# Fourier mixing and a squared-ReLU MLP: the second side of each block transposed one step later, and another end for the last block

## The chip, the cores and the metric

The kernel runs on one core of a Trainium2 chip. The metric is the device time of one execution in microseconds (us), lower is better. Results were compared with the reference.

Engines: PE is TensorE, PEld its weight loads, DVE is VectorE, ACT is ScalarE, POOL is GpSimd, SP is SyncE. A "q" after the name means the engine's instruction queue, which issues DMAs and waits.

## The reference

```python
def _attn_ref(x):                      # x: (8, 3008, 256) float32
    X = np.fft.fft(x, axis=1)
    X = np.fft.fft(X, axis=2)
    return X.real.astype(np.float32)

def _moe_ref(x, w_in, w_out):          # x: (24064, 256), w_in: (256, 2048), w_out: (2048, 256)
    h = x @ w_in
    r = np.maximum(h, 0.0)
    g = r * r
    return (g @ w_out).astype(np.float32)
```

## The kernel before

The kernel uses symmetry: row k and row S-k of a batch are computed together, as two "sides" of one block of up to 251 positions k. There are 48 blocks (8 batches of 6). Each takes 8 steps; a step makes hidden features (`front`: tiles ph), squares them, and multiplies them with the second weights (`back`: seven products into four accumulators mA to mD, a fast 2x2 scheme). While one batch goes through, the folds and DFT products (tiles pd) of the next are slipped in between as side work.

After the eighth step `gather` forms the two sides in `c`, and two steps later `store` transposes them to rows and writes them out:

```python
    psd = ctx.enter_context(tc.tile_pool(name="psd", bufs=2, space=PSUM))   # tag "d": pd tiles AND po tiles
    ...
    def gather(n):
        ...
        nc.scalar.copy(sA[:, :, 0:n], mA[:, :, 0:n])
        nc.scalar.copy(sB[:, :, 0:n], mB[:, :, 0:n])
        m1, m2, m4, m5 = sA[:, 0, 0:n], sA[:, 1, 0:n], sB[:, 0, 0:n], sB[:, 1, 0:n]
        ...
        tt(out=u2, in0=m1, in1=mC[:, 0, 0:n], op=ALU.add)          # VectorE
        tt(out=u3, in0=u2, in1=mC[:, 1, 0:n], op=ALU.add)
        tt(out=u4, in0=u2, in1=mD[:, 0, 0:n], op=ALU.add)
        gt = nc.gpsimd.tensor_tensor
        gt(out=c[:, 0, 0, 0:n], in0=m1, in1=m2, op=ALU.add)        # GpSimd
        gt(out=c[:, 1, 0, 0:n], in0=u3, in1=m4, op=ALU.subtract)
        gt(out=c[:, 1, 1, 0:n], in0=u3, in1=m5, op=ALU.add)
        gt(out=c[:, 0, 1, 0:n], in0=u4, in1=m5, op=ALU.add)
        return c

    def store(b, k0, n, c):
        m = (n + 1) // 2
        starts = (0, n - m)
        ...
        for s, (row, lo, hi) in enumerate(...):                     # both sides, one after the other
            po = psd.tile([P, 2, D], F32, name="po", tag="d")
            for i, o in enumerate(starts):
                for h in range(2):
                    nc.tensor.transpose(po[0:m, i, h * H:(h + 1) * H], c[:, s, h, o:o + m], ident)
            os_ = op.tile([P, 2, D], F32, name="os", tag="os")
            nc.scalar.copy(os_[0:m], po[0:m])
            for i, (o, c0, c1) in enumerate(((0, lo, m), (starts[1], m, hi))):
                nc.sync.dma_start(out=out[row + c0:row + c1], in_=os_[c0 - o:c1 - o, i])
    ...
    for i in range(len(steps) + LAG + 3):
        ...  front of step i, with side work between
        while finished and finished[0][0] <= i:
            store(*finished.pop(0)[1:])
        ...  back of step i - LAG
            if at[3] == NJ - 1:
                finished.append((i + 2, *at[:3], gather(at[2])))
```

## Time and profile before

| | before |
|---|---|
| time, median of 6 runs | 2067.1 us (2064.0 to 2071.0) |
| span of the profiled run | 2062.1 us |
| PE busy | 2004.4 us, 97% |
| PE's idle waits for ScalarE at the transposes | 10.1 us in 15 waits |
| first row of transposes to the last product | 1903.8 us |
| last product to the end of the span | 11.6 us |

The last two rows divide the span into the part that PE fills and the tail after it. What comes before the first transposes (the start: weights are loaded and converted) took 146.7 us in this run and isn't touched by the change.

### The profile page before, as it was taken

The numbers are of one execution on the slowest core, as the hardware profiler recorded it, in microseconds if no ns is written. First come the engines' busy times: TensorE is split into PE (matmuls) and PEld (weight loads), VectorE is DVE, ScalarE is ACT, GpSimd is POOL, SyncE is SP. The second block draws the span as 40 slices with busy tenths as digits, with TensorE's granted clock in tenths as the row PEclk, the third lists the DMA queues.
The fourth block names the chain that finished last, engine by engine and source line by source line (L and its number), as shares of the span: only waits on it lengthen the run. The fifth ranks groups of instructions, "written<-read, shape, count | busy, mean of one in ns | idle before, by whom it ended". The sixth has DMA issues, their size and how long they took to land.

```text
span 2062.1 us, 27082 instructions
## 1 busy us (share of the span) xinstructions
PE 2004.4 (97%) x9464; PEld 1742.7 (85%) x9464; DVE 1335.1 (65%) x3271; ACT 949.4 (46%) x1069; POOL 1204.8 (58%) x1766
## 2 busy tenths in 40 slices
PE   6699999999999999999999999999999999999997
PEld 4588888888888888888888888888888888888887
DVE  6898666776567755677557765677656775555553
ACT  1554444444444544454444444444444454445443
POOL 0376555666556654676557664666655665456565
PEclk9899999999999999999999999999999999999999
DMA  6232000110011010011001100011001100000000
GB/s 177 92 69 49 21 11 31 41 36 21 11 41 41 26 31 25 26 38 39 11 26 36 38 28 11 30 41 36 21 11 40 41 11 21 26 11 11 21 11 20
DMA packets 66104, 68.45 MB, mean 33 GB/s; under 512 B 26297, under 2 KB 56969, under 8 KB 65968
## 3 DMA queue, kind: packets, MB, share of 16 engines
q1 hardware_dynamic: 65152, 66.46, 11.3%
q8 instruction: 74, 1.21, 0.2%
q14 instruction: 62, 0.51, 0.1%
q10 hardware_dynamic: 816, 0.26, 0.1%
HBM read 42.03 MB, written 24.68 MB: 32 GB/s over the span
## 4 chain that ended last, share of the span: by engine, by line
PE 95%; DVE 3%; DMA 1%; ACT 1%; issue 0%; POOL 0%; POOLq 0%; SPq 0%; ACTq 0%; DVEq 0%
PE ph L405 16%; PE mA L445 16%; PE mC L445 16%; PE ph L406 16%; PE mB L445 16%; PE mD L445 8%; PE pd L345 5%; PE po L479 2%; PE pg L229 1%; DMA xt<-in_x_dram 1%; ACT os L481 0%; DVE he L408 0%; DVE fd L211 0%; DVE fs L213 0%; DVE g L411 0%
## 5 line engine op out<-in xcount | busy, mean ns | idle before, releaser
L419 ACT ACTIVATE g<-g 128x1004 f32<-128x1004 f32 (+1 forms) x384 | 399.4, 1040 | 829.3 <-DVE g L411 554.8
L408 DVE SCALAR_TENSOR_TENSOR he<-Et,gE,ph 128x251 f32<-128x251 f32 (+1 forms) x768 | 362.1, 472 | 590.2 <-PE ph L406 589.7
L425 POOL TENSOR_TENSOR s<-g 128x251 f32<-128x251 f32 (+1 forms) x384 | 251.5, 655 | 683.3 <-ACT g L420 656.6
L405 PE MATMUL ph<-Pt,G 128*128 128x251 f32 (+1 forms) x1536 | 452.5, 375 | 0.4 <-DVE g L411 0.4
L406 PE MATMUL ph<-Qt,G 127*128 127x251 f32 (+1 forms) x1536 | 451.2, 374 | 0.0
L420 ACT ACTIVATE g<-g 128x1004 f32<-128x1004 f32 (+1 forms) x384 | 399.3, 1040 | 12.2
L445 PE MATMUL mA<-g,wout 128*128 128x251 f32 (+1 forms) x1536 | 389.4, 375 | 0.0
L445 PE MATMUL mC<-s,wsum 128*128 128x251 f32 (+1 forms) x1536 | 389.4, 374 | 0.0
L410 DVE TENSOR_TENSOR g<-he,ph 128x251 f32<-128x251 f32 (+1 forms) x768 | 320.6, 417 | 58.9 <-DVE he L408 0.5
L405 PEld LDWEIGHTS ph<-Pt,G 128*128 128x128 f32 x1536 | 287.8, 189 | 42.2 <-issue 3.2
L406 PEld LDWEIGHTS ph<-Qt,G 127*128 127x128 f32 x1536 | 291.2, 190 | 35.8
L445 PEld LDWEIGHTS mC<-s,wsum 128*128 128x128 f32 x1536 | 291.6, 190 | 35.2
L445 PEld LDWEIGHTS mA<-g,wout 128*128 128x128 f32 x1536 | 285.0, 189 | 39.7 <-issue 4.0
L411 DVE TENSOR_TENSOR g<-he,ph 128x251 f32<-128x251 f32 (+1 forms) x768 | 314.2, 409 | 0.0
L426 POOL TENSOR_TENSOR s<-s,g 128x251 f32<-128x251 f32 (+1 forms) x384 | 288.8, 752 | 30.1
L427 POOL TENSOR_TENSOR s<-g 128x251 f32<-128x251 f32 (+1 forms) x384 | 290.2, 756 | 0.0
L428 POOL TENSOR_TENSOR s<-g,s 128x251 f32<-128x251 f32 (+1 forms) x384 | 264.2, 688 | 0.0
L445 PE MATMUL mB<-g,wsum 128*128 128x251 f32 (+1 forms) x768 | 225.2, 374 | 0.0
L445 PE MATMUL mD<-s,wout 128*128 128x251 f32 (+1 forms) x768 | 225.0, 374 | 0.0
L445 PE MATMUL mB<-s,wout 128*128 128x251 f32 (+1 forms) x768 | 224.6, 374 | 0.0
L445 PEld LDWEIGHTS mB<-g,wsum 128*128 128x128 f32 x768 | 145.6, 190 | 17.7
L445 PEld LDWEIGHTS mD<-s,wout 128*128 128x128 f32 x768 | 144.9, 189 | 18.1
(73 smaller groups left out, 1317.1 us busy)
## 6 DMA issues: line engine op xcount, KB each, us to landing
xt<-in_x_dram SPq DMA_DIRECT2D x24, 512.0 KB
out_dram<-os SPq DMA_DIRECT2D x96, 125.0 KB
out_dram<-os SPq DMA_DIRECT2D x80, 126.0 KB
xt<-in_x_dram SPq DMA_DIRECT2D x16, 384.0 KB
Et<-e_dram SPq DMA_DIRECT2D x7, 752.5 KB
raw<-in_moe_w_in_dram SPq DMA_DIRECT2D x16, 256.0 KB
raw<-in_moe_w_out_dram SPq DMA_DIRECT2D x16, 256.0 KB
xt<-in_x_dram SPq DMA_DIRECT2D x8, 480.0 KB
```

The source lines that it names most:

```text
L405: nc.tensor.matmul(hP, G1[:, fs], pt[:, ks], start=True, stop=True)
L406: nc.tensor.matmul(hQ, G2[:, fs], qt[:, ks], start=True, stop=True)
L408: nc.vector.scalar_tensor_tensor(out=t, in0=et[:, ks], scalar=gE[:, fc:fc + 1], in1=hP, op0=ALU.mult, op1=ALU.add)
L410: tt(out=g[:, h, 0, 0:n], in0=t, in1=hQ, op=ALU.add)
L411: tt(out=g[:, h, 1, 0:n][:, ::-1], in0=t, in1=hQ, op=ALU.subtract)
L419: act(v, v, AF.Relu)
L420: act(v, v, AF.Square)
L425: gt(out=s1, in0=g21, in1=g22, op=ALU.add)
L426: gt(out=s2, in0=s1, in1=g11, op=ALU.subtract)
L427: gt(out=s3, in0=g11, in1=g21, op=ALU.subtract)
L428: gt(out=s4, in0=g12, in1=s2, op=ALU.subtract)
L445: nc.tensor.matmul(acc[nm][:, i, 0:n], w, v[:, 0:n], start=j == 0 and i == 0, stop=j == NJ - 1, skip_group_check=True)
```

## The change

The intent: no longer let PE wait in the middle of the transposes, and shorten the chain after the last product, when nothing else is left to hide it. There are two independent parts.

Part one gives each side its own entry, so that side two is transposed one step after side one:

```diff
-                finished.append((i + 2, *at[:3], gather(at[2])))
+                c_ = gather(at[2], final)
+                finished += [(i + 2 + s, *at[:3], s, c_, final) for s in range(2)]
```

Part two concerns the last block only (`final`). Its last step makes mB's products at the end; VectorE adds mB straight from PSUM in place of GpSimd with a copy; ScalarE copies side one and issues its stores itself, VectorE copies side two, and the sync engine issues those stores:

```diff
+        if final and j == NJ - 1:
+            products = products[0:2] + products[4:7] + products[2:4]
...
-        nc.scalar.copy(sB[:, :, 0:n], mB[:, :, 0:n])
+        if not final:
+            nc.scalar.copy(sB[:, :, 0:n], mB[:, :, 0:n])
...
         gt(out=c[:, 0, 0, 0:n], in0=m1, in1=m2, op=ALU.add)
+        if final:
+            tt(out=c[:, 0, 1, 0:n], in0=u4, in1=mB[:, 1, 0:n], op=ALU.add)
+            tt(out=c[:, 1, 1, 0:n], in0=u3, in1=mB[:, 1, 0:n], op=ALU.add)
+            tt(out=c[:, 1, 0, 0:n], in0=u3, in1=mB[:, 0, 0:n], op=ALU.subtract)
+            return c
...
-            nc.scalar.copy(os_[0:m], po[0:m])
+        (nc.vector.tensor_copy if final and s else nc.scalar.copy)(os_[0:m], po[0:m])
-                nc.sync.dma_start(out=out[row + c0:row + c1], in_=os_[c0 - o:c1 - o, i])
+            (nc.scalar if final and not s else nc.sync).dma_start(out=out[row + c0:row + c1], in_=os_[c0 - o:c1 - o, i])
```

More of the change, by code (lines that the diff above doesn't have):

```diff
@@ L431, with back @@
     acc = {}
-    def back(n, j, g, s):
+    def back(n, j, g, s, final):
         if j == 0:
@@ L437, in back, with gather @@
                 acc[nm] = psm.tile([P, 2, CH], F32, name=nm, tag=nm)
-        for nm, i, w, v in (("mA", 0, wout[:, 0, j, 0:H], g[:, 0, 0]),
-                            ("mA", 1, wout[:, 1, j, 0:H], g[:, 1, 0]),
-                            ("mB", 0, wsum[:, 2, j], g[:, 1, 1]),
-                            ("mB", 1, wout[:, 0, j, H:D], s[:, 0]),
-                            ("mC", 0, wsum[:, 0, j], s[:, 1]),
-                            ("mC", 1, wsum[:, 1, j], s[:, 2]),
-                            ("mD", 0, wout[:, 1, j, H:D], s[:, 3])):
+        products = [("mA", 0, wout[:, 0, j, 0:H], g[:, 0, 0]),
+                    ("mA", 1, wout[:, 1, j, 0:H], g[:, 1, 0]),
+                    ("mB", 0, wsum[:, 2, j], g[:, 1, 1]),
+                    ("mB", 1, wout[:, 0, j, H:D], s[:, 0]),
+                    ("mC", 0, wsum[:, 0, j], s[:, 1]),
+                    ("mC", 1, wsum[:, 1, j], s[:, 2]),
+                    ("mD", 0, wout[:, 1, j, H:D], s[:, 3])]
+        if final and j == NJ - 1:
+            products = products[0:2] + products[4:7] + products[2:4]
+        for nm, i, w, v in products:
             nc.tensor.matmul(acc[nm][:, i, 0:n], w, v[:, 0:n], start=j == 0 and i == 0, stop=j == NJ - 1,
                              skip_group_check=True)
-    def gather(n):
+    def gather(n, final):
         mA, mB, mC, mD = (acc[nm] for nm in ("mA", "mB", "mC", "mD"))
@@ L467, in gather, with store @@
         return c
-    def store(b, k0, n, c):
+    def store(b, k0, n, s, c, final):
         m = (n + 1) // 2
         starts = (0, n - m)
-        first, last = k0 == 0, k0 + n == NKT
-        for s, (row, lo, hi) in enumerate(((b * S + k0, 0, n),
-                                           (b * S + S - (k0 + n - 1), 1 if last else 0, n - 1 if first else n))):
-            po = psd.tile([P, 2, D], F32, name="po", tag="d")
-            for i, o in enumerate(starts):
-                for h in range(2):
-                    nc.tensor.transpose(po[0:m, i, h * H:(h + 1) * H], c[:, s, h, o:o + m], ident)
-            os_ = op.tile([P, 2, D], F32, name="os", tag="os")
-            nc.scalar.copy(os_[0:m], po[0:m])
-            for i, (o, c0, c1) in enumerate(((0, lo, m), (starts[1], m, hi))):
-                nc.sync.dma_start(out=out[row + c0:row + c1], in_=os_[c0 - o:c1 - o, i])
+        if s == 0:
+            row, lo, hi = b * S + k0, 0, n
+        else:
+            row, lo, hi = b * S + S - (k0 + n - 1), 1 if k0 + n == NKT else 0, n - 1 if k0 == 0 else n
+        po = psd.tile([P, 2, D], F32, name="po", tag="d")
+        for i, o in enumerate(starts):
+            for h in range(2):
+                nc.tensor.transpose(po[0:m, i, h * H:(h + 1) * H], c[:, s, h, o:o + m], ident)
+        os_ = op.tile([P, 2, D], F32, name="os", tag="os")
+        (nc.vector.tensor_copy if final and s else nc.scalar.copy)(os_[0:m], po[0:m])
+        for i, (o, c0, c1) in enumerate(((0, lo, m), (starts[1], m, hi))):
+            (nc.scalar if final and not s else nc.sync).dma_start(out=out[row + c0:row + c1], in_=os_[c0 - o:c1 - o, i])
     def ahead(b):
@@ L558 @@
     flight, finished = [], []
-    for i in range(len(steps) + LAG + 3):
+    for i in range(len(steps) + LAG + 4):
         if i < len(steps):
@@ L578 @@
             at, g_, s_ = flight.pop(0)
-            back(at[2], at[3], g_, s_)
+            final = at[:3] == (B - 1, *BLOCKS[-1])
+            back(at[2], at[3], g_, s_, final)
             if at[3] == NJ - 1:
-                finished.append((i + 2, *at[:3], gather(at[2])))
+                c_ = gather(at[2], final)
+                finished += [(i + 2 + s, *at[:3], s, c_, final) for s in range(2)]
         if i < len(steps):
```

## The prediction

> **What bounds the kernel now.** I read the page first: busy shares, then the chain that ended last. TensorE (PE) is the bound.
>
> ```profile
> span 2062.1 us, 27082 instructions
> ...
> PE 2004.4 (97%) x9464; PEld 1742.7 (85%) x9464; DVE 1335.1 (65%) x3271; ACT 949.4 (46%) x1069; POOL 1204.8 (58%) x1766
> ...
> PE 95%; DVE 3%; DMA 1%; ACT 1%; issue 0%; POOL 0%; POOLq 0%; SPq 0%; ACTq 0%; DVEq 0%
> ```
>
> PE is busy 97% of the span and is 95% of the chain. The change removes no matmul, so it can win only where PE stands still, or after PE's last stream. The second view is PE's own waits (line waited for: us in total, times, longest).
>
> ```profile
> PE pg L229 <- DVE win L214: 28.8, 7, 12.0
> PE po L479 <- ACT os L481: 10.1, 15, 0.7
> PE po L479 <- POOL c L466: 2.5, 1, 2.5
> ```
>
> The 28.8 us belong to the conversion of weights at the start; the change doesn't touch them. The other two lines are what it aims at: 15 waits of the transposes (po) for ScalarE's copy of a transposed side (os), and one wait in the tail. The third view is the timeline of one of the 15 (start, length, instruction, idle time before it).
>
> ```profile
> 519.67 0.60 PE L479 MATMUL po<-ident,c 128*126 128x128 f32 x4
> ...
> 520.30 0.59 ACT L481 COPY os<-po 126x512 f32<-126x512 f32 x1 [1.65 <-PE po L479]
> ...
> 520.94 0.66 PE L479 MATMUL po<-ident,c 128*126 128x128 f32 x4 [0.68 <-ACT os L481]
> ...
> 521.44 1.01 PE L445 MATMUL mA<-g,wout 128*128 128x251 f32 x4
> ```
>
> Four transposes, a whole copy of 0.59 us during which PE does nothing, four more. From the first transpose to the first matmul after them is 521.44 - 519.67 = 1.77 us. In a block without the wait eight transposes stand in one row: 400.02 us to the matmul at 400.89 us, 0.87 us. So a stalled block loses 0.90 us, more than the 0.68 us of idle time that the wait view prints: the four transposes after the wait start slower too, and the drain before it isn't counted as idle.
>
> The fourth view is the timeline of the tail.
>
> ```profile
> 2049.92 0.58 PE L445 MATMUL mD<-s,wout 128*128 128x250 f32 x2
> ...
> 2050.19 0.42 DVE L459 TENSOR_TENSOR u<-sA,mC 128x250 f32<-128x250 f32 x1 [6.87 <-PE mC L445]
> ...
> 2051.20 0.63 POOL L464 TENSOR_TENSOR c<-u,sB 128x250 f32<-128x250 f32 x1 [1.40 <-DVE u L460]
> ...
> 2052.45 0.63 POOL L466 TENSOR_TENSOR c<-u,sB 128x250 f32<-128x250 f32 x1
> ...
> 2053.14 1.03 PE L479 MATMUL po<-ident,c 128*125 128x128 f32 x7 [2.52 <-POOL c L466]
> 2053.77 1.07 ACT L481 COPY os<-po 125x512 f32<-125x512 f32 x2 [3.92 <-PE po L479]
> 2054.38 1.58 SPq L483 DMA_DIRECT2D out_dram<-os  x4
> ```
>
> PE's products end at 2050.50. Then three VectorE sums, three GpSimd sums, transposes, two copies, four stores; the first store is issued at 2054.38. The last view is the DMA from 2055 to 2061 us.
>
> ```profile
> DMA packets 518, 0.51 MB, mean 85 GB/s; under 512 B 19, under 2 KB 518, under 8 KB 518
> ## 3 DMA queue, kind: packets, MB, share of 16 engines
> q1 hardware_dynamic: 518, 0.51, 27.9%
> ```
>
> 27.9% of 16 engines for 6 us is 26.8 us of engine time, 52 ns a packet. The packets run from 2055.14 to 2060.88, 5.74 us, so on average 4.7 engines worked, and the rest none.
>
> **What the Trainium skill says.** "PSUM — Partial Sum Buffer", section Specifications (TRN2): 8 banks of 2 KiB per partition. The kernel holds two ph, four m and two "d" tiles, each a bank: all eight. A third buffer for the transposes can't be had, so the change spreads them in time instead. "DMA: Bandwidth & Descriptors", section "Why a DMA increments its semaphore by 16 and not by 1": the number of engines of a transfer is the largest k up to 16 that divides its slowest dimension. The last stores have three times 125 rows and once 124: k = 5 and 4. The trace agrees: engines 0 to 3 would have 3x25+31 data packets and 4 for the semaphores, 110 x 52 ns = 5.7 us, and the 5.74 us were measured. The same page, section "Issuing engines are not separate DMA queues": transfers issued by different engines run on the same 16 DMA engines, and a second issuer saves sequencer time only. Nothing in the profile of before has two issuers in the tail, so that isn't shown yet. "VectorE: DVE Perf Modes", section on the TRN2 errata: 120 cycles plus one per element for PSUM to SBUF, 658 ns for 512 columns. The trace's VectorE rows that read PSUM take 414 ns at 251 columns and 548 at 377, 1.06 ns a column: by that line 691 ns at 512, which I use.
>
> **The change, part by part.**
> *Side two one step later.* In the built program of before, the stalled second side waits for ScalarE because a DFT group's tile (pd) holds the other of the two "d" buffers across it. In the changed one a whole step, 11 pairs of products, lies between the sides. A step is 4.67 us (mA to mA, 2036.80 to 2041.47); the copy needs about 0.04 + 0.59 us. So the buffer is long free. The same eight transposes run per block. Gain: 15 x 0.90 = 13.4 us, all of it PE's time. Cost of splitting one row of eight into two rows of four: the first start-to-start distance in a row is 112 ns, the others 109, and the product after the row follows 109 ns after the last transpose; 47 x 0.003 us = 0.1 us.
>
> *Products reordered in the last step.* mC and mD come before mB. Each pair takes 0.42 us, so the same sum is shifted: mC ends at 2049.23 instead of 2050.08, mD at 2049.66, mB at 2050.50. Their inputs s were there at 2048.30, in time.
>
> *Sums.* VectorE starts u2 about 0.11 us after mC, as before: 2049.34; u3 0.45 later (dependent) at 2049.79; u4 0.33 later at 2050.12. The first c needs mB's end: 2050.50 + 0.11 = 2050.61, done 2051.03; the next two follow at 0.33 us: done 2051.36 and 2051.69. Before, the last c of side one was done at 2053.08. The gain is 2.05 us for side one. The GpSimd sums (0.63 to 0.71 us each, after u3 alone) and the copy sB drop out.
>
> *Copies and stores.* From c to ScalarE's copy was 0.68 us (2053.08 to 2053.77), so its copy of side one starts at 2051.71, ends at 2052.30, and its own queue issues at about 2052.33, against 2054.38. Side two: transposes from 2051.75, 0.70 us as above, VectorE's copy 2052.5 to 2053.2, stores by the sync engine at 2053.2 and 2053.6. Before, the second copy ended at 2054.84.
>
> *Stores' transfer.* The four have the same rows on the same few engines, about 5.7 us of work that starts 0.76 us after the first issue and has no gap, since the second pair comes (2053.6 + 0.8 = 2054.4) while the first pair's 2.6 us last (to 2055.7). So the end moves by what the first issue moves: 2.05 us. The 1.2 us from the last packet to the end stay.
>
> Sum: -13.4 + 0.1 - 2.05 = -15.4 us, and 2065.7 - 15.4 = 2050.3 us, 0.75% less.
>
> **The rivals.**
> *The wait comes back elsewhere.* The buffer that side two used to grab is now taken by the DFT's last product, which in the built order waits for ScalarE's copy of side one, where it waited for VectorE before. If that stalled as long, the gain of part one would shrink to nothing, and the time be 2063.5. Against it: seven products and a first ph pair, 3.8 us, lie between, and the copy is done 0.63 us after the transposes. VectorE is another candidate (it runs 65% busy, and the DFT's joins are its work), but PE waited 0.4 us for it at ph in the whole run. I give a loss of more than half one chance in twelve.
> *Weights become the limit at the row's edges.* Small DFT products start 250 ns apart instead of their streaming time, because the weight load takes 0.2 us. If each additional row of transposes cost 0.1 us so, 47 rows would take back 4.7 us: 2055. Against it: the second four of a stalled block are followed by mA at 109 ns already.
> *The tail's stores overlap.* If 52 ns a packet is latency that two queues can overlap, the transfer shrinks by up to half for the part in which both have work: up to 2 us more, 2048.3. For it speaks that one queue has never more than one packet an engine in flight on average; against it the skill's sentence.
> *The tail gains nothing.* ScalarE's DMA issues at the start took 0.42 to 0.49 us against 0.26 to 0.34 of the sync engine later. That is 0.2 us, no more.
>
> **Range and chances.** The stalls are counted and regular, so part one is good to about 1 us; the tail to 1 us; the three runs of before span 3.3 us. Predicted 2050.3 us; 2047.3 to 2053.6 should hold it 8 times in 10. 2% is 41 us: all idle time of PE is 58 us, half of it at the start and untouched, so neither faster nor slower by 2% has more than 1 chance in 100.
>
> **What would show it right or wrong.** Right: PE's wait of po for os is gone from 15 to 0; every row of transposes has four and takes 0.44 us; PE's busy time falls by a few us at most while the span falls by 15; the first store is issued about 2.05 us sooner after the last product; the DMA stretch still lasts 5.7 us at 4.7 engines. Wrong: a new line of pd waiting for ACT os, ph waiting for DVE, a DMA stretch of under 5 us, or a granted clock below 0.99.

## The result, and the profile after

The changed kernel took 2050.8 us in the median of 6 runs (2048.9 to 2057.4), the kernel before 2067.1 us. The ratio is 0.9925 with a 95% interval of 0.9908 to 0.9942: 0.75% less. A ratio here is the mean time of one kernel's runs over that of the other's in the same rounds, so it isn't quite the ratio of the medians. All outputs are right.

The waits of PE after the change (line waited for: us in total, times, longest), with the start's wait again on top:

```profile
PE pg L229 <- DVE win L214: 28.7, 7, 11.9
...
PE po L490 <- DVE c L470: 0.5, 1, 0.5
```

The 15 waits of po for ScalarE's os are gone, and neither pd waiting for os nor more waiting of ph for VectorE has come in their place (ph L405 waits 0.4 us in both). What is left at po is one wait in the tail, for VectorE's sum. The block shown in the prediction now looks like this on PE (start, length, instruction):

```profile
519.78 0.60 PE L490 MATMUL po<-ident,c 128*126 128x128 f32 x4
520.22 1.01 PE L448 MATMUL mA<-g,wout 128*128 128x251 f32 x4
...
524.04 2.06 PE L345 MATMUL pd<-cosT,wP 128*128 128x376 f32 x6
...
526.79 0.60 PE L490 MATMUL po<-ident,c 128*126 128x128 f32 x4
527.23 0.80 PE L448 MATMUL mA<-g,wout 128*128 128x251 f32 x3
```

Two rows of four transposes, each 0.44 us to the next product (520.22 - 519.78 and 527.23 - 526.79), 0.87 us together, what an undisturbed row of eight took before. Between them lies a step, with a DFT product in it. The product (pd) now takes the buffer that side two used to queue for, and PE goes on without a gap.

The tail after the change:

```profile
2038.94 0.42 DVE L464 TENSOR_TENSOR u<-sA,mC 128x250 f32<-128x250 f32 x1 [6.02 <-PE mC L448]
...
2039.51 0.58 PE L448 MATMUL mB<-s,wout 128*128 128x250 f32 x2
...
2040.23 0.42 DVE L470 TENSOR_TENSOR c<-u,mB 128x250 f32<-128x250 f32 x1
...
2040.71 1.41 PE L490 MATMUL po<-ident,c 128*125 128x128 f32 x7 [0.50 <-DVE c L470]
...
2041.34 0.59 ACT L492 COPY os<-po 125x512 f32<-125x512 f32 x1 [2.73 <-PE po L490]
...
2041.95 0.86 ACTq L494 DMA_DIRECT2D out_dram<-os  x2
2042.16 0.69 DVE L492 COPY os<-po 125x512 f32<-125x512 f32 x1 [0.86 <-PE po L490]
2042.88 0.72 SPq L494 DMA_DIRECT2D out_dram<-os  x2
```

The last product ends at 2040.10 (2039.51 + 0.58, rounded), the first store is issued at 2041.95, 1.85 us later; before it was 3.87 us (2050.50 to 2054.38). The stores' packets, over 6 us as in the prediction (2042.7 to 2048.7):

```profile
DMA packets 518, 0.51 MB, mean 85 GB/s; under 512 B 19, under 2 KB 518, under 8 KB 518
...
q1 hardware_dynamic: 258, 0.26, 14.5%
q10 hardware_dynamic: 260, 0.26, 14.1%
```

The sum of the two queues, 28.6% of 16 engines, is about that of the one queue before (27.9%), and the transfer lasts as long as before (5.80 us against 5.74). The second queue's packets begin at 2045.15, the first's end at 2045.48: the two work one after the other nearly throughout.

Where the 15 us went, from the two traces:

| | before | after | difference |
|---|---|---|---|
| start, to the first row of transposes | 146.74 | 149.67 | +2.93 |
| first transposes to the end of the last product | 1903.76 | 1890.42 | -13.34 |
| last product to the first store's issue | 3.87 | 1.85 | -2.02 |
| first issue to the first packet | 0.76 | 0.81 | +0.05 |
| first packet to the last | 5.74 | 5.80 | +0.06 |
| last packet to the end | 1.24 | 1.23 | -0.01 |

The first line is scatter, not the change: PE's first mA product began between 89.2 and 95.6 us in the twelve traces, none of whose edits touches the start. It hides 3 us of the gain between these two spans (2062.1 and 2049.8 us). The other lines sum to -15.26 us. PE's busy time is 2004.4 us in both.

### The profile page after: what moved, and what is told of

Same layout as the page of the kernel before. It is cut to its first block, busy times and chain, and to the rows that moved or that the text cites. A ratio compares the mean times of both kernels' runs of the same rounds, so it can differ in the third digit from the quotient of the medians.

```text
span 2049.8 us, 27083 instructions
## 1 busy us (share of the span) xinstructions
PE 2004.4 (98%) x9464; PEld 1743.8 (85%) x9464; DVE 1337.7 (65%) x3275; ACT 952.2 (46%) x1067; POOL 1203.9 (59%) x1763
## 4 chain that ended last, share of the span: by engine, by line
PE 95%; DVE 3%; DMA 1%; issue 0%; SPq 0%; ACT 0%; DVEq 0%
PE ph L405 16%; PE mA L448 16%; PE ph L406 16%; PE mC L448 16%; PE mB L448 16%; PE mD L448 8%; PE pd L345 5%; PE po L490 2%; PE pg L229 1%; DMA xt<-in_x_dram 1%; DVE he L408 0%; DVE g L411 0%; PE pe L235 0%; DVE g L410 0%; DMA raw<-in_moe_w_in_dram 0%
## 5 line engine op out<-in xcount | busy, mean ns | idle before, releaser
L405 PE MATMUL ph<-Pt,G 128*128 128x251 f32 (+1 forms) x1536 | 452.4, 375 | 0.5 <-DVE g L411 0.4
L405 PEld LDWEIGHTS ph<-Pt,G 128*128 128x128 f32 x1536 | 287.8, 189 | 42.0 <-issue 3.2
```

What stands on the lines that cost most here:

```text
L405: nc.tensor.matmul(hP, G1[:, fs], pt[:, ks], start=True, stop=True)
```

## The experiments

My theory: part one is worth 0.90 us for each block whose second side waits for a buffer, 15 of 48, and nothing in the others; part two is worth what the first store is issued earlier, 2.0 us, because the transfer itself is bound by the few DMA engines that rows of 125 and 124 use. My rivals: the row of eight transposes, or two copies in one step, cost something in every block; and the second copy engine and the second queue are what shortens the tail. The edits are relative to the changed kernel, unless another is named.

One more rival has to be met: in the block shown in the prediction VectorE's last read of the DFT's tile (pd) ends at 520.86, only 0.03 us before ScalarE's copy (520.89), so the wait might be for VectorE. The block at 274.54 us of the kernel before separates the two:

```profile
275.18 0.59 ACT L481 COPY os<-po 126x512 f32<-126x512 f32 x1 [2.74 <-PE po L479]
...
275.82 0.66 PE L479 MATMUL po<-ident,c 128*126 128x128 f32 x4 [0.68 <-ACT os L481]
275.84 0.35 DVE L360 TENSOR_TENSOR dc<-pd,db 127x188 f32<-127x188 f32 x1
```

There PE goes on just after ScalarE's copy, while VectorE's last read of pd has yet to start. The program agrees: in 15 blocks side two is given side one's own buffer and waits for ScalarE.

### Each part alone (5 rounds each)

```diff
-            final = at[:3] == (B - 1, *BLOCKS[-1])
+            final = False
```

> The changed kernel with the last block's end left as it was before; only the second side is transposed one step later. Theory (15 stalls of 0.90 us, a tail worth 2 us): 13.4 us faster than before, ratio 0.9935; in the trace no wait of po for os on PE, and from PE's last product to the end 11.6 us as before. Rival (the tail does more than its traced 1.9 us, for instance because a start-up difference of 3 us hid part of it): under 11 us faster.

Part one alone: 2053.5 us, ratio 0.9934 (0.9922 to 0.9946). From the first transposes to the last product 1890.6 us, from there to the end 11.62 us.

```diff
-                finished += [(i + 2 + s, *at[:3], s, c_, final) for s in range(2)]
+                finished += [(i + 2, *at[:3], s, c_, final) for s in range(2)]
```

> The changed tail alone: both sides of every block transposed in the same step, as before. Theory: 2.0 us faster, ratio 0.999; the 15 waits of po for os on PE stay at 10 us in sum; from PE's last product to the end 9.7 us in place of 11.6 us. Rival (tail worth more, or the parts only work together): more than 4 us faster, or nothing.

Part two alone: 2064.5 us, ratio 0.9986 (0.9974 to 0.9998). Its waits still show what part one removes:

```profile
PE po L490 <- ACT os L492: 10.1, 15, 0.7
```

From the first transposes to the last product it took 1903.76 us, as before to the hundredth, and 9.71 us from there to the end. The two ratios multiply to 0.9920, against 0.9925 for both: the parts are independent, about 13.2 and 1.9 us by the traces (1903.76 - 1890.60 and 11.61 - 9.71).

### Half a step (5 rounds)

```diff
-                finished += [(i + 2 + s, *at[:3], s, c_, final) for s in range(2)]
+                finished += [(i + 2 + s / 2, *at[:3], s, c_, final) for s in range(2)]
+        while finished and finished[0][0] <= i + 0.5:
+            store(*finished.pop(0)[1:])
```

> The second side is transposed half a step after the first: right after the same step's seven products (2.97 us) in place of a whole step later (4.67 us). Theory (only the buffer's release matters: the copy is done 0.63 us after the first side's last transpose): the same time as the changed kernel within 1 us, no wait of po for os. Rival (what helps is that ScalarE's or the sync engine's work is spread over two steps): half of the gain or less, waits appear.

2051.8 us, ratio 0.9926 (0.9913 to 0.9939), no wait of po for os, and 1890.33 us from the first transposes to the last product. Seven products between the sides do as well as a whole step. ScalarE's two copies are again in the same step as before the change, so it isn't the spreading of its work that helps. This fits that the distance only has to be longer than the copy that frees the buffer (0.63 us after the last transpose); no distance between that and half a step was tried.

### Fewer waits by another place (5 rounds)

Both sides in one step again, without part two, but four steps after the gathering in place of two. Because the DFT's tiles are then held at other moments, 7 blocks collide with one, not 15:

```diff
-            final = at[:3] == (B - 1, *BLOCKS[-1])
+            final = False
-                finished += [(i + 2 + s, *at[:3], s, c_, final) for s in range(2)]
+                finished += [(i + 4, *at[:3], s, c_, final) for s in range(2)]
```

(The loop was made four rounds longer to match.)

> As before, both sides in one step and the old tail, but both two steps later than before. In the built order 7 blocks in place of 15 then have a second side that waits for ScalarE's copy. Theory (each such block costs 0.90 us, the others nothing): 7 waits, and 8 x 0.90 = 7.2 us faster than before, ratio 0.9965. Rival (the row of eight transposes itself costs in every block): the same time as before within 2 us.

2059.3 us, ratio 0.9962 (0.9949 to 0.9975), 7.9 us less by the ratio.

```profile
PE po L490 <- ACT os L492: 4.7, 7, 0.7
PE po L490 <- POOL c L476: 2.5, 1, 2.5
```

Seven waits, as counted in the built program. Here the first transposes stand two steps later, so the comparison starts at the first mA product: 1953.80 us from it to the last product, against 1961.34 before, 7.54 us less. Block by block, the 15 stalled rows of before lose about 0.895 us each (one of them 0.95), 13.5 in sum, and the 7 here 0.95 each, 6.7 in sum: 6.8 us less. The other 0.7 us lie between products elsewhere, and no run explains them. The row of eight costs nothing in the other blocks: it takes 0.874 us in all 40 that have no wait here, and two rows of four take 2 x 0.438 in the changed kernel. With 15, 7 and 0 waits the gain follows the count.

A by-product: this kernel's tail was 0.3 us longer than before (11.91 us). Its last seven transposes took 1.75 us of PE time in place of 1.03, and the granted clock was 0.56 in that stretch, where it was 1.00 in the kernel before. Both kernels let PE idle 2.5 us just before, waiting for GpSimd. In this one the record of the clock falls to 0.5 at 2047.02, 0.15 us after the transposes began; in the kernel before it falls at 2055.95, when they are long done. Why it falls at that moment, no run here shows.

### The tail taken apart (3 rounds each)

First the sums without the engines: both copies on ScalarE and all four stores on the sync engine.

```diff
-        (nc.vector.tensor_copy if final and s else nc.scalar.copy)(os_[0:m], po[0:m])
+        nc.scalar.copy(os_[0:m], po[0:m])
-            (nc.scalar if final and not s else nc.sync).dma_start(out=out[...], in_=...)
+            nc.sync.dma_start(out=out[...], in_=...)
```

> The changed kernel with both of the last block's copies on ScalarE and all four stores on the sync engine; VectorE's sums from PSUM and the new order of products stay. Theory (the stores' transfer is bound by the few DMA engines that 125 and 124 rows use, so only the first issue counts): first issue 1.9 us after PE's last product, transfer 5.7 to 5.8 us, from the last product to the end 9.7 us, as with the whole change. Rival (second copy engine and second queue are worth something): 10.2 us or more.

2050.8 us, ratio 0.9925 (0.9909 to 0.9941). First issue 1.85 us after the last product, transfer 5.72 us, 9.56 us to the end: 0.13 us less than with the whole change, whose tail took 9.67 to 9.71 us in three traces. The second copy engine and the second queue bring nothing; the first packet comes 0.81 us after the first issue in the five traces where ScalarE issues first with these rows, 0.76 in the five with the sync engine alone. The gain is in the sums; the order of the products, VectorE's reading from PSUM and the dropped copy were not tried apart.

Then the engines without the sums:

```diff
-            back(at[2], at[3], g_, s_, final)
+            back(at[2], at[3], g_, s_, False)
-                c_ = gather(at[2], final)
+                c_ = gather(at[2], False)
```

> The changed kernel with the last block's products and sums as before (GpSimd, from the copy sB); only the two copies and the stores go to two engines. Theory: the last sum comes as late as before, first issue 3.9 us after the last product, from there to the end 11.6 us, so this half of the tail's change is worth nothing alone. Rival: under 11.0 us.

2053.9 us, ratio 0.9942 (0.9922 to 0.9962), 12.39 us from the last product to the end. This was a miss: I had expected 11.6 us, no gain, and it is 0.8 us worse than the kernel before. The first issue was as expected, 3.88 us after the last product, but the transfer took 6.48 us. In this kernel both copies end close together, and the four stores are issued by ScalarE, sync, ScalarE, sync within 0.84 us; the two queues work at the same time. In the whole change, the sync engine's stores begin only as ScalarE's end (2045.15 and 2045.48 above).

### One queue or two (one look each)

```diff
-            (nc.scalar if final and not s else nc.sync).dma_start(out=out[...], in_=...)
+            nc.sync.dma_start(out=out[...], in_=...)
```

(to the kernel with the engines alone)

> The end with only the two copies on two engines had a transfer of 6.5 us in place of 5.7 us, which nothing had foretold. Here both copies stay on two engines, but all four stores are issued by the sync engine in one queue, one side after the other. If the interleaving of two queues cost the 0.7 us: transfer 5.7 to 5.8 us, from the last product to the end 11.6 us. If it was the copies or chance of that execution: 6.4 us again.

Transfer 5.75 us, 11.61 us from the last product to the end.

> The same kernel as the one with only the two copies and queues split, once more. If interleaved queues cost it: transfer 6.2 to 6.8 us again, with both queues at work at the same time. If that execution was an odd one: 5.8 us.

Transfer 6.45 us, 12.37 us to the end. So it wasn't chance, nor the copies: the two queues cost 0.7 us here when their stores alternate on the same DMA engines (6.45 and 6.48 us, against 5.72 to 5.76 in the five traces with one queue). In both executions the last 0.8 us of the transfer had fewer than two packets in flight on average (1.4, against 2.5 with the one queue of before), so the engines seem to have finished unevenly; why, no run here shows.

### Other row counts for the last stores

If the transfer is bound by the number of DMA engines, other row counts must change it. The last block's pieces overlap as transposes (128 columns from the start and the last 128) but not as stores:

```diff
+        if final:
+            m, starts = P, (lo, n - P)
+            pieces = ((0, lo, lo + P), (1, lo + P, lo + P + 112), (1, lo + P + 112, hi))
+        else:
+            pieces = ((0, lo, m), (1, m, hi))
...
-        for i, (o, c0, c1) in enumerate(((0, lo, m), (starts[1], m, hi))):
+        for i, c0, c1 in pieces:
+            o = starts[i]
```

> The whole change, and the last block's 250 and 249 rows are transposed and stored as 128 + 112 + the rest in place of 125 + 125 (124): the same bytes in six stores, whose row counts 128 and 112 divide by 16. Theory (the number of DMA engines of a store follows from its rows): the transfer takes 2.0 to 2.7 us in place of 5.8 us with the packets' mean time near 52 ns, from the last product to the end 6.0 to 6.6 us in place of 9.7 us, 3 to 3.7 us faster than the change. Rival (the transfer is bound by bytes or by the issue of descriptors on a queue): 5 us or more for the transfer, nothing gained.

2046.5 us (2045.4 to 2047.6, 4 runs), ratio 0.9902 (0.9888 to 0.9917): the best kernel. It is 4.3 us under the changed one's median and as much under that of the sums alone, measured beside it; 3.5 us of this is the tail by the traces, the rest is no more than the scatter of the start. Its stores in the window 2040.0 to 2044.7:

```profile
DMA packets 582, 0.51 MB, mean 109 GB/s; under 512 B 83, under 2 KB 582, under 8 KB 582
```

The transfer takes 2.16 us in place of 5.80, and 6.22 us pass from the last product to the end in place of 9.69. The column "under 512 B" tells why: these are the 4-byte writes to semaphores, one for each DMA engine of each store. Here there are 83 = 16 + 16 + 10 + 16 + 16 + 9; with 125, 125, 125 and 124 rows there were 19 = 5 + 5 + 5 + 4.

The opposite test stores 127 + 123 and 127 + 122 rows (one look, relative to the kernel just above):

```diff
-            pieces = ((0, lo, lo + P), (1, lo + P, lo + P + 112), (1, lo + P + 112, hi))
+            pieces = ((0, lo, lo + P - 1), (1, lo + P - 1, hi))
```

> As the kernel with 128 + 112 + rest rows, but the last block is stored as 127 + 123 and 127 + 122 rows. Theory (the number of engines is the largest divisor of the rows up to 16, always the lowest-numbered engines: 1, 3, 1 and 2): engine 0 has 127 + 41 + 127 + 61 = 356 packets of 52 ns, transfer 18 to 19 us, from the last product to the end 22 to 23 us. Rival (fewer engines only by accident of 125): 6 us or less for the transfer.

```profile
DMA packets 506, 0.51 MB, mean 31 GB/s; under 512 B 7, under 2 KB 506, under 8 KB 506
```

7 = 1 + 3 + 1 + 2 semaphore writes, as foretold, and the same bytes in 16.23 us, 20.11 us from the last product to the end. The expectation had the right engine counts and a transfer too long, 18 to 19 us. It took the mean of 52 ns for the time of every packet. In the last microsecond of this transfer, one packet follows the other every 42 ns and takes 46; 46 is also the median in the other traces, and some 30 to 70 slower packets of each transfer, up to 0.46 us, raise the mean. The tail is 10.4 us longer than the whole change's: two unlucky row counts in one block of 48 give back two thirds of what the change won.

## Why the prediction was right

The time lay in the range (2050.8 us against 2050.3 predicted), and by its steps:

- *Part one, -13.4 + 0.1 us.* The traces show -13.34 us with both parts and -13.16 with this one alone. That a stalled block loses 0.90 us and not the 0.68 us of the wait view was the step that mattered: the waits sum to 10.1 us only. The distance from the first transpose to the product after the row is the measure. In a stalled row the fifth transpose starts 0.95 us after the fourth in place of 0.11, and the sixth 0.16 after the fifth, also in place of 0.11: 0.89 in sum. The idle time begins only when the fourth transpose has ended, 0.27 us after its start, and so leaves 0.2 us out. The count is confirmed by the kernel with 7 waits, the cause by the half step.
- *No wait comes back, and the extra rows cost nothing.* Both rivals fell: no new line in PE's waits, and 0.44 us for each row of four. (The first rival's time should have read 2063.7, 2050.3 + 13.4, and not 2063.5.)
- *Sums.* The first store was issued 2.02 us sooner relative to the last product; 2.05 was predicted. VectorE's copy of 512 columns took 0.69 us, as extrapolated.
- *Transfer.* It stayed at 5.8 us and moved with the first issue. The terms that were slightly mis-sized: ScalarE's first store reached its first packet after 0.81 us where I carried over the sync engine's 0.76, and the transfer took 5.80 us in place of 5.74. So the tail gave 1.92 us, not 2.05.
- *What the prediction didn't say:* that the second half of part two is not merely worthless but costs 0.13 us, and costs 0.8 us where the queues alternate. It named as a rival that two queues might overlap and gain; it didn't think of a loss.

The sum of parts by trace is -15.3 us. The medians differ by 16.3 us, the ratio gives 15.5; the start's scatter is that large. So that the median came within 0.5 us of the number is partly luck: the prediction started from 2065.7, the median of the first three runs before, and six gave 2067.1. What speaks for the mechanism is the agreement part by part in the traces.

## What to carry to other kernels

When two short-lived tiles and a long-lived one share two buffers, look for the moments at which the long one is alive; moving the second short tile past its predecessor's release removes the wait (half a step and a whole one both did here), at no cost where the engine has other work to put between. Size such a wait from start to start of the work around it, not from the idle time alone. And look at the row counts of the last stores before giving them a second queue: 128 + 112 + 10 rows went out in 2.2 us where twice 125 a side took 5.8.

## What the Trainium skill lacked or had wrong

- "DMA: Bandwidth & Descriptors", section "Why a DMA increments its semaphore by 16 and not by 1": its rule for the number of engines held in all the row counts tried (semaphore writes 19, 83 and 7 as computed from it). What it lacks is a time for a transfer on few engines: the same 0.51 MB took 2.2, 5.8 or 16.2 us here.
- The same page, section "Issuing engines are not separate DMA queues": it says that a second issuing engine saves only sequencer time. No gain is what the runs show too (9.56 us for one queue, 9.69 for two); that alternating two queues can cost time, 6.5 us in place of 5.75 for the same stores, it doesn't say.
- "VectorE: DVE Perf Modes", section on the TRN2 errata: by an estimate from its table, a float32 copy of 512 columns from PSUM takes 658 ns; 0.69 us was measured.
